# The experts' first product by seven block products, in three passes of 768 tokens

## The chip, the cores and the metric

The kernel runs on one core of one Trainium2 chip. The metric is the device time of one execution in microseconds (us). TensorE (PE in the profile) multiplies, with its weight loads listed as PEld; VectorE (DVE), ScalarE (ACT) and GpSimd (POOL) do the elementwise work; SyncE (SP) issues most of the DMAs.

## What is computed

Three layers run one after another on 2304 tokens (4 sequences of 576) of width 512. The reference, cut to what matters:

```python
# retention, 8 heads of 64
scores = q @ k.T / 8
x = (scores * where(rel >= 0, gamma[h] ** rel, 0)) @ v          # [2304, 512]
# first feed-forward (its weights come as float64)
h = x @ w_in                                                    # [2304, 1024]
e = exp(h - max(h)); sm = e / (sum(e) + 1e-9)
solu = h * sm
ln = (solu - mean) / sqrt(var + 1e-6) * g_ln
x = ln @ w_out                                                  # [2304, 512]
# second feed-forward, 4 experts, each w1 [512, 1024] and w2 [1024, 512]
for e in range(4):
    out += p[:, e] * (relu(x @ w1[e]) @ w2[e])
```

## The kernel before

Every large product keeps float32 accuracy with three matmuls in the float32r format: each operand is split into a high part (a copy rounded by ScalarE) and a low part (operand minus high part, on VectorE or GpSimd), and `mm3` (lines 99 to 103) issues high x high, high x low and low x high. TensorE loads a 128x128 stationary tile for each of them and streams 384 or 512 columns.

The tokens go in two halves of 1152 (9 groups of 128, 3 blocks of 384). For each half the stages are:

- Retention of a group (`att_*`): scores `att_qk` (line 262), decay mask `att_ret` (VectorE, line 269), keys x values `att_st` (279), running state `att_state` (VectorE, 296 and 298), outputs `att_pv` (314 to 325), split of the outputs `att_x`. Scaled values (line 231) and scaled queries (248, 249; for some groups of the opening on VectorE, 242) come before. The 1 MB of a group lies in one of two buffers (two more at the very start), and the load of group g+2 waits until the outputs of group g have read theirs.
- First projection of a group: `h_mm` (24 matmuls of 512 columns into `hps`), then `chain1` to `chain3` (maximum 356, exp 359, softmax and moments 368 and 372, norm 383), then eight transposes `t_mm` (403) with a split.
- `x2_mm`: for a block of 384 tokens and each of four 128-column pieces, 24 matmuls of 384 columns.
- The experts: in each of `nsteps` = 96 steps of a half, `l1` makes one 128-row piece of the hidden layer for one block (12 matmuls of 384 columns, relu and split on ScalarE 441 and VectorE 442), and `l2`, two steps behind, adds one piece to three output tiles (9 matmuls of 512 columns); after eight pieces `l2_out` scales by the expert's probability and adds to the sum (457, 459).

The float64 weights w_in and w_out are decoded in 16 chunks at the start (`dec_pre` on ScalarE 159 and 160, `dec_dve` on VectorE 164 to 172, `dec_pool` on GpSimd 176 and 177), split, and their float32 value is also stored to DRAM (`scr`, ScalarE's DMA queue), from where the second half loads and splits them again. The experts' weights are loaded and split in each half (`w_split`).

The order of the first part is written out by hand in `ORDER`: it covers the retention and the first projection of the first half and the decoding of all 16 chunks. The first `x2_mm` follows it. The second half's retention is spread between its first projections (`step`), with the first two groups inside the first half's last expert steps. Engines run their instructions in the order of the program. PSUM has two buffers of 1024 columns (`psA`: `hps`, the output tiles) and four of one bank (`psB`: everything else).

Of the kernel before, what the change touches and what calls it, by code (L numbers as in the profile page):

```python
# [10 lines left out]
F32R = mybir.dt.float32r  # L11
AF = mybir.ActivationFunctionType
# [11 lines left out]
HALF = NT // 2  # L24
GH = HALF // P
BLK = 384
NB = HALF // BLK
TB = BLK // P
KD = DM // P
KF = FF // P  # L30
NJ = 9
TABW = 1024 + 512 + NJ * H + NJ * NP + 128
U32 = mybir.dt.uint32
# [13 lines left out]
R0 R1 A0 P0 P1 C1 D0 A1 D1 G0 C0 K0 R2 G1 B0 A2 E0 E1 P2 V2 J0 v1 Q2 q1 K1 v0 R3 J1 R4 P3 S1 D2 S0 U0 G2 R5 O0  # L47
U1 K2 O1 D3 A3 X0 G3 J2 P4 e2 X1 S2 D4 E3 A4 G4 O2 Q3 U2 H0 K3 R6 X2 P5 V3 D5 P6 K4 R7 q4 J3 D6 G5 A5 R8 J4 V4
G6 H2 P7 S3 e4 S4 D7 V5 E5 U3 O3 E6 U4 O4 S5 X3 G7 P8 D8 Q5 X4 R9 E7 K5 H1 A6 R10 V6 P9 J5 O5 Q6 P10 U5 K6 N0
G8 H3 D9 S6 J6 X5 M0 G9 A7 O6 H4 C2 R11 K7 H5 N1 q7 M1 F0 U6 v7 S7 Z0 X6 E8 F1 E9 A8 I0 R12 J7 D10 O7 G10 Q8  # L50
P11 N2 U7 D11 v8 X7 T0 H6 K8 E10 S8 R13 G11 P12 H7 U8 P13 R14 M2 J8 I1 N3 O8 F2 D12 T1 X8 H8 H9 I2 M3 E11 F3
N4 D13 T2 H10 H11 P14 I3 M4 G12 N5 F4 M5 R15 D14 T3 G13 E12 H12 F5 I4 H13 N6 H14 P15 I5 M6 H15 D15 G14 G15 T4
F6 E13 E14 N7 E15 H16 M7 I6 F7 T5 I7 H17 N8 M8
# [4 lines left out]
def retention_solu_moe(  # L58
# [15 lines left out]
    wp = ctx.enter_context(tc.tile_pool(name="wp", bufs=8))  # L74
    stp = ctx.enter_context(tc.tile_pool(name="stp", bufs=2))
    drp = ctx.enter_context(tc.tile_pool(name="drp", bufs=1, space=bass.MemoryType.DRAM))
    bdp = ctx.enter_context(tc.tile_pool(name="bdp", bufs=2))
    ap2 = ctx.enter_context(tc.tile_pool(name="ap2", bufs=2))
    xp = ctx.enter_context(tc.tile_pool(name="xp", bufs=4))
    ep = ctx.enter_context(tc.tile_pool(name="ep", bufs=3))  # L80
    lp = ctx.enter_context(tc.tile_pool(name="lp", bufs=1))
    x2p = ctx.enter_context(tc.tile_pool(name="x2p", bufs=3))
    accp = ctx.enter_context(tc.tile_pool(name="accp", bufs=1))
# [13 lines left out]
    mhalf = const.tile([P, 1], F32, name="mhalf")  # L97

    def mm3(ps, lhs, rhs, first, last):
        (lh, ll), (rh, rl) = lhs, rhs  # L100
        nc.tensor.matmul(ps, lh, rh, start=first, stop=False)  # L101
        nc.tensor.matmul(ps, lh, rl, start=False, stop=False)  # L102
        nc.tensor.matmul(ps, ll, rh, start=False, stop=last)  # L103

    def split(dst_hi, dst_lo, src, scale=None):
        if scale is None:
            nc.scalar.activation(out=dst_hi, in_=src, func=AF.Copy)  # L107
            nc.vector.tensor_tensor(out=dst_lo, in0=src, in1=dst_hi.bitcast(F32), op=ALU.subtract)  # L108
        else:
            nc.scalar.activation(out=dst_hi, in_=src, func=AF.Copy, scale=scale)  # L110
            nc.vector.scalar_tensor_tensor(
                out=dst_lo, in0=src, scalar=scale, in1=dst_hi.bitcast(F32), op0=ALU.mult, op1=ALU.subtract
            )

# [1 line left out]
    scr = [drp.tile([P, 512], F32, name=f"scr{i}") for i in range(16)]  # L116
    mixed = [("A", 0), ("A", 1)] + [x for i in range(6) for x in (("A", i + 2), ("B", i))] + [("B", 6), ("B", 7)]
    worder = []
    for half in range(2):
        first = [("A", i) for i in range(8)] + [("B", i) for i in range(8)]  # L120
        for kind, i in first if half == 0 else mixed:
            worder.append((kind, scr[i] if kind == "A" else scr[8 + i]))
        for e in range(E):
            for kind, i in first if e == 0 else mixed:
                worder.append((kind, w1[e, i] if kind == "A" else w2[e, i]))
    wstate = {"dma": 0, "cut": 16}
    wstage = {}
    wtiles = {"A": {}, "B": {}}
    wcount = {"A": 0, "B": 0}
    dec = []  # L130

    def w_load():
        i = wstate["dma"]
        if i >= len(worder):
            return
        wstate["dma"] = i + 1
        if i < 16:
            if i == 0:
                dec.append(x2p.tile([P, 3072], F32, tag="x2", name="dec_raw"))
                dec.append(x2p.tile([P, 3072], F32, tag="x2", name="dec_w0"))  # L140
                dec.append(x2p.tile([P, 3072], F32, tag="x2", name="dec_w1"))
# [579 lines left out]
```

## Time and profile before

| | us |
|---|---|
| median of 3 runs (1137.45 to 1139.17) | 1137.88 |
| span of the profiled execution | 1137.7 |
| PE busy | 1102.1 (97%) |
| PEld busy | 990.7 (87%) |
| DVE busy | 452.4 (40%) |
| ACT busy | 327.2 (29%) |
| POOL busy | 98.9 (9%) |

Busy time is the time in which an engine has an instruction in execution. Matmuls overlap one another, so what one costs is read from the distance between starts, not from its duration. The timeline lists starts and durations, the chain of waits lists the pieces that set the end, the view by line groups instructions and gives the mean of one, and the view by stretches gives busy times, granted TensorE clock, DMA share and rate in a stretch.

### The profile page before, as it was taken

The page shows a single profiled execution, that of the slowest core. Times are in us where ns is not written, and L with a number is a line of the kernel's source. Part 1 is how long each engine was busy: PE and PEld are TensorE (multiplying, and loading weights), DVE is VectorE, ACT ScalarE, POOL GpSimd, SP SyncE. Part 2 cuts the span into 40 slices and gives each one's busy share as a digit, 9 for nine tenths or more (in the row PEclk, how much of TensorE's full clock was granted, in tenths as well). Part 3 has the DMA queues.
Part 4 walks back from the last instruction along what each step waited for, and adds up shares of the span by engine and source line. Part 5 has one row for each costly group of instructions (what it writes and reads, how often), then busy time and mean ns, then how long its engine had stood idle before and what let it go on. Part 6 is the DMA issues. An engine that isn't in the chain of part 4 may idle for free.

```text
span 1137.7 us, 14749 instructions
## 1 busy us (share of the span) xinstructions
PE 1102.1 (97%) x6176; PEld 990.7 (87%) x6176; DVE 452.4 (40%) x788; ACT 327.2 (29%) x613; POOL 98.9 (9%) x93
## 2 busy tenths in 40 slices
PE   4798999999999999999999999999999999999998
PEld 4676899999999999999877899999999999999997
DVE  6998743214223411432346635422431241233221
ACT  3456842113112311311134626311321131122110
POOL 4744500000000000000002200000000000000000
PEclk9899999999999999999999999999999999999999
DMA  8452012103101300211244300210220030021000
GB/s 327 178 211 76 38 48 68 35 1 111 37 1 38 111 1 1 94 55 65 84 149 158 112 1 11 84 56 1 74 74 1 19 112 19 1 74 57 28 29 28
DMA packets 31314, 75.82 MB, mean 67 GB/s; under 512 B 3728, under 2 KB 3728, under 8 KB 29072
## 3 DMA queue, kind: packets, MB, share of 16 engines
q1 hardware_dynamic: 28944, 70.69, 18.7%
q10 hardware_dynamic: 2304, 4.20, 1.0%
q8 instruction: 48, 0.79, 0.3%
q14 instruction: 18, 0.15, 0.0%
HBM read 65.96 MB, written 8.91 MB: 66 GB/s over the span
## 4 chain that ended last, share of the span: by engine, by line
PE 91%; DVE 7%; ACT 1%; POOL 0%; issue 0%; DMA 0%; POOLq 0%; DVEq 0%; ACTq 0%
PE l1ps L101 12%; PE l1ps L103 12%; PE o L102 12%; PE l1ps L102 12%; PE o L103 12%; PE o L101 12%; PE x2ps L101 3%; PE x2ps L102 3%; PE x2ps L103 3%; PE hps L101 2%; PE hps L102 2%; PE hps L103 2%; PE qk L262 1%; PE tps L403 1%; PE o L325 1%; PE o L314 1%
## 5 line engine op out<-in xcount | busy, mean ns | idle before, releaser
L442 DVE SCALAR_TENSOR_TENSOR hts<-l1ps,hts 128x384 fp32r<-128x384 f32 x192 | 107.0, 557 | 530.4 <-ACT hts L441 530.4
L441 ACT ACTIVATE hts<-l1ps 128x384 fp32r<-128x384 f32 x192 | 94.4, 492 | 608.8 <-PE l1ps L103 608.8
L103 PE MATMUL l1ps<-x,wA 128*128 128x384 f32 x768 | 258.9, 337 | 0.0
L101 PE MATMUL l1ps<-x,wA 128*128 128x384 f32 x768 | 258.7, 337 | 0.0
L102 PE MATMUL l1ps<-x,wA 128*128 128x384 f32 x768 | 257.9, 336 | 0.0
L103 PE MATMUL o<-wB,hts 128*128 128x512 f32 x576 | 227.8, 396 | 0.0
L102 PE MATMUL o<-wB,hts 128*128 128x512 f32 x576 | 227.4, 395 | 0.0
L101 PE MATMUL o<-wB,hts 128*128 128x512 f32 x576 | 224.0, 389 | 0.0
L101 PEld LDWEIGHTS l1ps<-x,wA 128*128 128x128 f32 x768 | 144.3, 188 | 8.3 <-issue 0.2
L102 PEld LDWEIGHTS l1ps<-x,wA 128*128 128x128 f32 x768 | 144.1, 188 | 7.8
L103 PEld LDWEIGHTS l1ps<-x,wA 128*128 128x128 f32 x768 | 144.0, 188 | 0.0
L103 PEld LDWEIGHTS o<-wB,hts 128*128 128x128 f32 x576 | 108.0, 188 | 23.0
L102 PEld LDWEIGHTS o<-wB,hts 128*128 128x128 f32 x576 | 108.0, 188 | 18.4
L101 PEld LDWEIGHTS o<-wB,hts 128*128 128x128 f32 x576 | 108.2, 188 | 17.5
L101 PE MATMUL hps<-wA,xt 128*128 128x512 f32 x144 | 60.1, 417 | 1.5 <-ACT hps L372 1.1
L102 PE MATMUL hps<-wA,xt 128*128 128x512 f32 x144 | 57.3, 398 | 0.0
L103 PE MATMUL hps<-wA,xt 128*128 128x512 f32 x144 | 57.2, 397 | 0.0
L108 DVE TENSOR_TENSOR wA<-wst,wA 128x512 fp32r<-128x512 f32 x72 | 49.6, 691 | 14.7 <-ACT wA L107 14.5
L108 DVE TENSOR_TENSOR wB<-wst,wB 128x512 fp32r<-128x512 f32 x72 | 51.1, 709 | 8.8 <-ACT wB L107 8.2
L231 POOL TENSOR_TENSOR grp<-grp,tabs 128x512 f32<-128x512 f32 x11 | 12.1, 1103 | 428.6 <-DMA grp<-in_qkv 428.6
L107 ACT ACTIVATE wA<-wst 128x512 fp32r<-128x512 f32 x72 | 44.8, 626 | 13.2 <-DMA wst<-in_w 6.6
L107 ACT ACTIVATE wB<-wst 128x512 fp32r<-128x512 f32 x72 | 45.1, 627 | 10.8 <-DMA wst<-in_w 7.3
(100 smaller groups left out, 1086.4 us busy)
## 6 DMA issues: line engine op xcount, KB each, us to landing
wst<-in_w SPq DMA_DIRECT2D x128, 256.0 KB, 2.6
grp<-in_qkv SPq DMA_DIRECT2D x15, 1024.0 KB, 5.0
dec_raw<-in_w_in SPq DMA_DIRECT2D x8, 512.0 KB, 6.0
scr<-dec_w ACTq DMA_DIRECT2D x16, 256.0 KB, 2.5
dec_raw<-in_w_out SPq DMA_DIRECT2D x8, 512.0 KB, 4.3
wst<-scr SPq DMA_DIRECT2D x16, 256.0 KB, 2.6
out<-accA SPq DMA_DIRECT2D x12, 256.0 KB, 2.0
lend<-in_qkv SPq DMA_DIRECT2D x2, 1024.0 KB, 8.1
```

The lines of the kernel that those rows point to most:

```text
L101: nc.tensor.matmul(ps, lh, rh, start=first, stop=False)
L102: nc.tensor.matmul(ps, lh, rl, start=False, stop=False)
L103: nc.tensor.matmul(ps, ll, rh, start=False, stop=last)
L107: nc.scalar.activation(out=dst_hi, in_=src, func=AF.Copy)
L108: nc.vector.tensor_tensor(out=dst_lo, in0=src, in1=dst_hi.bitcast(F32), op=ALU.subtract)
L231: eng.tensor_tensor(out=vd, in0=v, in1=vtab[:, j].unsqueeze(2).to_broadcast([P, H, 64]), op=ALU.mult)
L262: nc.tensor.matmul(qk[a][:, n], kt[r, n], qt[r, n], start=True, stop=True)
L314: nc.tensor.matmul(o[r, n, 0:cross], v[:, 2 * n + a], ret[:, a, n, 0:cross], start=n == 0, stop=j == 0 and n == NP - 1)
L325: nc.tensor.matmul(o[:, n, 0:cross], st[:, n], qd[:, n, 0:cross], start=False, stop=n == NP - 1)
L403: nc.tensor.transpose(ps[:, f], y[:, (4 * u + f) * P : (4 * u + f + 1) * P], ident)
L441: nc.scalar.activation(out=ht[:, 0], in_=ps, func=AF.Relu)
L442: nc.vector.scalar_tensor_tensor(out=ht[:, 1], in0=ps, scalar=0.0, in1=ht[:, 0].bitcast(F32), op0=ALU.max, op1=ALU.subtract)
```

## The change

The tokens go in three passes of 768 (6 groups, two blocks of 384 tokens, b = 0 and 1).

- Experts' first product: the product x @ w1 of a pass is cut into 2x2 blocks (512 hidden inputs in two halves, tokens in two blocks, hidden units m and m+4) and made by seven block products instead of eight, with sums and differences of blocks. The blocks of w1 are laid out in advance (a21, a11, a12, a22); GpSimd makes four combined blocks s1 to s4 of each step (`w1_ops`), ScalarE and VectorE or GpSimd split everything. The four combined blocks of x (T1 to T4) are made behind `x2_mm`. The seven products of a step share three PSUM tiles x, y and z; partial sums are copied out by ScalarE (t1r, t2r, t5r) and added by VectorE.
- A step has 7 products of 6 matmuls (384 columns); an expert has 4 steps, then all of `l2` for six output tiles (24 matmuls of 512 columns each).
- `ORDER` now holds the retention of all 18 groups, the decoding of all 16 chunks and the first projection of 6 groups. The outputs of groups 6 to 17 are split and stored to DRAM (`att_store`, SP queue, 512 KB each) and loaded in their pass.
- The decoded weights are stored as two parts (512 KB a chunk instead of 256 KB) after the low part is made, and loaded again as parts in passes 1 and 2 (`next_loads`, and eight loads of wB). All low parts of decoded weights, all scaled values and the second factor of all scaled queries are on GpSimd; none of them is on VectorE.
- w2 is split by ScalarE and GpSimd inside the steps, w1 mostly behind `l2`.

```diff
+NPASS = 3
+GP = NG // NPASS
+TB = GP // 2
...
+    def low(dst, src, hi, eng=None):
+        (eng or nc.vector).tensor_tensor(out=dst, in0=src, in1=hi.bitcast(F32), op=ALU.subtract)
...
+    def dec_lo(i):
+        t = dec_out(i)
+        low(t[:, 1], dec_views(i)[4], t[:, 0], nc.gpsimd)
+
+    def dec_store(i):
+        nc.scalar.dma_start(out=(s_in if i < 8 else s_out)[i % 8], in_=dec_out(i).bitcast(F32))
...
+    def grp(g):
+        return grps[:, 3072 * (g % 2) : 3072 * (g % 2) + 3072]
...
+    def att_store(g):
+        if g >= GP:
+            nc.sync.dma_start(out=s_x[g], in_=att_to(g).bitcast(F32))
...
+    PRODUCTS = {1: (A11, B11), 2: (A12, B21), 3: (S4, B22), 4: (A22, T4), 5: (S1, T1), 6: (S2, T2), 7: (S3, T3)}
...
+    def prod(s, i, bank, more=False):
+        a, b = PRODUCTS[i]
+        for kk in range(2):
+            mm3(
+                bank, (wpart(s, a, kk, 0), wpart(s, a, kk, 1)), (xpart(b, kk, 0), xpart(b, kk, 1)),
+                not more and kk == 0, kk == 1, more,
+            )
...
+        if i == 1:
+            prod(s, 1, x)
+            copy(t1r, x)
+            if m > 0:
+                relu_hi(1, m + 3, c22)
+                relu_lo(1, m + 3, c22)
+        elif i == 5:
+            prod(s, 5, y)
+            copy(t5r, y)
+        elif i == 2:
+            prod(s, 2, z)
+            add(z, z, t1r)
+        elif i == 6:
+            prod(s, 6, x, True)
+            copy(t2r, x)
+            relu_hi(0, m, z)
+            relu_lo(0, m, z)
+        elif i == 3:
+            prod(s, 3, y, True)
+            add(y, y, t2r)
+        elif i == 7:
+            prod(s, 7, x, True)
+            add(c22, x, t5r)
+            relu_hi(1, m, y)
+            relu_lo(1, m, y)
...
+        elif i == 4:
+            prod(s, 4, x, True)
+            relu_hi(0, m + 4, x)
+            relu_lo(0, m + 4, x)
...
+            for m in range(NM):
+                s = s0 + m
+                for i in (1, 5, 2, 6, 4, 3, 7):
+                    if i != 4:
+                        l1(s, i)
+                    elif m > 0:
+                        l1(s - 1, 4)
...
+            for b in (1, 0):
+                for t in range(TB):
...
+                    l2_out(p, e, b * TB + t, ps)
+                    run(bg, 6)
```

In the new `ORDER` the letters are: R, A, C loads; P, D, G, E, e decoding and split of a weight chunk, W its store; V, Q, q, K, J, S, U, O, X, x the retention of a group and y its store; H, N, n, M, m, F, f, I, T, t, u first projection, norm and transposes. Its last part is the retention of groups 14 to 17 and the transposes of groups 3 and 4.

## Rows read from the trace of the kernel before

**Rows 1.** The page: span, and busy time of each engine.

```profile
span 1137.7 us, 14749 instructions
PE 1102.1 (97%) x6176; PEld 990.7 (87%) x6176; DVE 452.4 (40%) x788; ACT 327.2 (29%) x613; POOL 98.9 (9%) x93
```

**Rows 2.** Timeline of PE in an expert step: start us, duration us, instruction.

```profile
300.43 0.39 PE L101 MATMUL o<-wB,hts 128*128 128x512 f32 x1
...
302.51 0.33 PE L101 MATMUL l1ps<-x,wA 128*128 128x384 f32 x1
...
304.62 0.39 PE L101 MATMUL o<-wB,hts 128*128 128x512 f32 x1
```

**Rows 3.** Stretches: from:to length, busy us (instructions) per engine, clock, DMA.

```profile
0.00:133.40 133.40, 103.80 (x764) 85.65 (x765) 115.16 (x202) 75.65 (x132) 72.26 (x65) 0.94 0.48 175
30.00:60.00 30.00, 22.31 (x199) 18.66 (x197) 29.46 (x41) 12.86 (x26) 20.52 (x16) 0.79 0.51 178
180.00:570.00 390.00, 390.00 (x1998) 353.74 (x1997) 116.84 (x191) 79.49 (x155) 2.25 (x2) 1.00 0.16 50
```

**Rows 4.** Chain of waits: start us, us, what; opening, then a group of the second half.

```profile
59.46 0.43 PE hps L102
...
98.99 0.87 PE tps L403 x8
...
100.10 0.23 PE hps L102
...
600.17 1.09 PE qk L262 x16
601.26 0.62 PE st L279 x16
...
604.86 1.02 PE o L314 x16
605.89 1.09 PE o L325 x8
...
609.73 1.09 PE qk L262 x16
```

**Rows 5.** By line, opening to 133.4 us, DVE: instruction xcount | busy us, mean ns.

```profile
L269 DVE TENSOR_TENSOR ret<-qk,tabs 128x512 f32<-128x512 f32 x18 | 11.5, 680 | 0.0
L368 DVE SCALAR_TENSOR_TENSOR ex<-hps,rs,ex 128x1024 f32<-128x1024 f32 x8 | 10.3, 1284 | 0.3
L356 DVE TENSOR_REDUCE nm<-hps 128x1 f32<-128x1024 f32 x8 | 9.7, 1218 | 2.3 <-PE hps L103 2.2
L242 DVE SCALAR_TENSOR_TENSOR grp<-grp,tabs 128x128 f32<-128x128 f32 x12 | 6.3, 583 | 0.0
L298 DVE TENSOR_TENSOR st<-st,st 64x256 f32<-64x256 f32 x12 | 5.0, 418 | 0.1
```

**Rows 6.** Stretches, DVE's instructions on the decoding's tile alone: busy us (instructions).

```profile
5.00:7.05 2.05, 1.92 (x5) 1.00 0.89 278
0.00:133.40 133.40, 52.74 (x70) 0.94 0.48 175
```

**Rows 7.** Timeline of all engines, 7 to 9 us.

```profile
7.16 1.31 POOL L176 TENSOR_TENSOR dec_w<-dec_w 128x512 f32<-128x512 f32 x1 [5.41 <-DVE dec_w L172]
7.26 1.49 DVE L166 TENSOR_SCALAR dec_w<-dec_raw 128x512 uint32<-128x512 uint32 x1
```

**Rows 8.** By line, opening to 133.4 us, POOL.

```profile
L195 POOL TENSOR_TENSOR wB<-dec_w,wB 128x512 fp32r<-128x512 f32 x7 | 9.0, 1291 | 14.2 <-ACT wB L194 14.2
L249 POOL TENSOR_TENSOR grp<-grp,tabs 128x512 f32<-128x512 f32 x3 | 4.0, 1340 | 0.2 <-ACT grp L248 0.2
```

**Rows 9.** DMA issues of the opening: KB each, us from issue to landing.

```profile
grp<-in_qkv SPq DMA_DIRECT2D x6, 1024.0 KB, 6.1
```

**Rows 10.** Timelines of DVE and ACT, one group's norm in the second half.

```profile
690.27 1.23 DVE L356 TENSOR_REDUCE nm<-hps 128x1 f32<-128x1024 f32 x1 [1.75 <-PE hps L103]
697.48 0.19 ACT L372 ACTIVATION_READ_ACCUMULATOR hps<-ex,mu 128x1 f32 x1
```

**Rows 11.** The page: the costliest group of DVE, the hidden layer's low part.

```profile
L442 DVE SCALAR_TENSOR_TENSOR hts<-l1ps,hts 128x384 fp32r<-128x384 f32 x192 | 107.0, 557 | 530.4 <-ACT hts L441 530.4
```

More of the change, by code (lines that the diff above doesn't have):

```diff
@@ L116, in retention_solu_moe @@
[L116 to L141, printed above, removed]
[L142 to L147 removed]
+    states = [const.tile([P, NP, P], F32, name=f"st{i}") for i in range(2)]
@@ new lines, in retention_solu_moe, with mm3 @@
+    s_in = [drp.tile([P, 1024], F32, name=f"sin{i}") for i in range(8)]
+    s_out = [drp.tile([P, 1024], F32, name=f"sout{i}") for i in range(8)]
+    s_x = [drp.tile([P, 1024], F32, name=f"sx{i}") for i in range(NG)]
+    def mm3(ps, lhs, rhs, first, last, more=False):
+        (lh, ll), (rh, rl) = lhs, rhs
+        nc.tensor.matmul(ps, lh, rh, start=first, stop=False, skip_group_check=more)
+        nc.tensor.matmul(ps, lh, rl, start=False, stop=False, skip_group_check=more)
+        nc.tensor.matmul(ps, ll, rh, start=False, stop=last, skip_group_check=more)
@@ new lines, in t_to, with t_hi, t_lo, tr @@
+    def t_to(g, part, u):
+        b, j = divmod(g % GP, TB)
+        return hT[b][:, part, 4 * u : 4 * u + 4, j * P : (j + 1) * P]
+    def t_hi(g):
+        for u in range(2):
+            copy(t_to(g, 0, u), tps[g][u])
+    def t_lo(g):
+        for u in range(2):
+            low(t_to(g, 1, u), tps[g][u], t_to(g, 0, u))
+    def tr(g):
+        t_mm(g)
+        t_hi(g)
+        t_lo(g)
+    B11, B21, B22, T1, T2, T3, T4 = range(7)
+    def xpart(b, kk, part):
+        return xv[0][:, b, kk, part] if b < 4 else xv[1][:, b - 4, kk, part]
@@ L487, in weights, with l2_mm @@
-    def weights(kind, at):
-        return {i: wtiles[kind].get(at + i) for i in range(8)}
+            nc.vector.scalar_tensor_tensor(out=a, in0=ps, scalar=sc, in1=a, op0=ALU.mult, op1=ALU.add)
+        if e == E - 1:
+            nc.sync.dma_start(out=out[tok * P : (tok + 1) * P, :], in_=a)
+    FORDER = [0, 4, 1, 5, 2, 6, 3, 7]
+    def l2_mm(ps, b, t, fs, first, last):
+        sl = slice(t * P, t * P + P)
+        for f in fs:
+            h, w = hT[b], wB[:, f]
+            mm3(
+                ps, (h[:, 0, f, sl], h[:, 1, f, sl]), (w[:, 0], w[:, 1]),
+                first and f == fs[0], last and f == fs[-1],
+            )
@@ new lines, in retention_solu_moe @@
+        for atom in ORDER.split():
+            atoms[atom[0]](int(atom[1:]))
+        second(0, None)
+        experts(0)
+        for p in range(1, NPASS):
+            g0 = p * GP
+            for i in range(8):
+                nc.sync.dma_start(out=wB[:, i].bitcast(F32), in_=s_out[i])
+            for i in range(GP):
+                g = g0 + i
+                h_mm(g, 0)
+                h_mm(g, 1)
+                chain1(g)
+                chain1e(g)
+                if i > 0:
+                    chain3a(g - 1)
+                if i > 1:
+                    tr(g - 2)
+                if i > 0:
+                    chain3m(g - 1)
+                    chain3b(g - 1)
+                chain2(g)
+                chain2s(g)
+            second(p, g0)
+            experts(p)
```

664 lines of the change are left out of this document (302 added, 362 removed).

## The prediction, made before the change was built

> **What bounds the kernel now.** I read the page first: TensorE is busy for 1102.1 of 1137.7 us, every other engine for under half of it apart from its own weight loads [rows 1]. Busy time does not say what a matmul costs, so the next view is the timeline of an expert step: the nine 512-column matmuls from 300.43 to 302.51 take 2.08 us, 0.231 each, the twelve 384-column ones from 302.51 to 304.62 take 2.11, 0.176 each, with no gap [rows 2]. The stretches come third: from 180 to 570 us TensorE is busy in all of 390 us at full clock while VectorE has 116.8 and GpSimd 2.3 [rows 3]. So after the opening the time is the sum of the matmul distances, and a matmul left out is 0.176 us won. The opening, up to the first `x2_mm` at about 133.4 us, is another stage: TensorE is busy for 103.8 us (overlaps counted once) and VectorE for 115.2 of 133.4 [rows 3]; from 30 to 60 us VectorE has 29.5 of 30 while TensorE has 22.3 at a granted clock of 0.79. There VectorE sets the pace.
>
> **The change, part by part.** The sum is made against the span of 1137.7 us, which stands 0.2 us below the median of the runs.
>
> *Matmuls left out.* Before, a hidden piece of a block takes 12 matmuls, 192 pieces, 2304 in all. After, 3 passes x 4 experts x 4 steps x 7 products x 6 = 2016 of the same shape, with a new stationary tile for each as before. 288 x 0.176 = -50.6 us. The second products, `x2_mm`, first projections and transposes keep their number and shape.
>
> *Work that changes sides of the opening's end.* Retention costs TensorE 1.09 + 0.61 + 1.02 + 1.09 = 3.81 us a group at full clock [rows 4]. The last nine groups leave the PE-bound second half for the opening: -34.3 after it. Three first projections of 24 matmuls at 0.23 and one set of transposes of 0.87 [rows 4] go the other way: +16.6 + 0.9. With the matmuls left out, what comes after the opening shrinks by 50.6 + 34.3 - 17.5 = 67.4 us. All else hangs on how long the opening gets.
>
> *The opening's length.* VectorE's 115.2 us change as follows [rows 5]: 18 more masks at 0.68 (+12.2), 9 more low parts of outputs, also 128x512 from PSUM, at the same 0.68 (+6.1), 16 more state updates at 0.42 (+6.7); gone are twelve scaled-query instructions (-6.3), three scaled values and six low parts of weights, 128x512 again (-6.1), and two groups' maximum and softmax at 1.22 and 1.28 (-5.0). Net +7.6, 122.8 us. GpSimd gets what VectorE lost and more: 11 scaled values and 11 query products at 1.34, 7 low parts at 1.29 [rows 8], 72.3 + 38 = 110 us.
> That matters because VectorE's decoding instructions get longer beside GpSimd: an L166 that starts during a GpSimd instruction takes 1.49 us [rows 7], while the first chunk's four, with nothing beside them, take 1.92 together. All DVE work on the decoding's tile is 52.7 us [rows 6]; less the six low parts, 48.6, against 16 x 1.92 = 30.7 alone: 17.9 us of waiting at a GpSimd share of 72.3/133.4 = 0.54. With 110 us in about 150 the share is 0.73 and the waiting 24.2: +6.3, so VectorE has 129.1. Bounds: no added waiting, or every one of the 64 instructions 1.01 longer than alone (1.49 against a quarter of 1.92), 65 of waiting, +47; I take the scaled value, since the share is the only thing that changes.
> Before, the opening lasted 133.4/115.2 = 1.158 times VectorE's work (it starts late and ends with a chain). Kept, this gives 149.5 us. `ORDER` now ends with the last groups' chain with little beside it, scores, mask and outputs of some 4 us of which part is extra: I add 3. Opening: 153 us, against 133.4: +19.6.
> (The Trainium skill, page "SBUF — State Buffer", section "Who interferes with whom", says that the engine that comes second is blocked for the whole of the other's instruction. Rows 7 agree. By it alone, an estimate: 64 instructions x 0.73 x half of a 1.3 us instruction = 30 us of waiting instead of 24, and the sum would be 7 us higher, 1104.)
>
> *What else could set the opening.* ScalarE has 75.7 us before; 44 more short query copies and 9 output copies, all taken at 0.68 or less, make at most 112. Each W on its queue now waits for GpSimd's low part (1.29) with the Q and X copies queued behind it: 16 x 1.29 = 21 at most, 133, still under 153; I take none of it on the path, and all of it in the range. DMA: 0.48 of the engines carried 175 GB/s, 23 MB [rows 3]; 9 more groups (9.4 MB), larger weight stores (4.2) and 12 output stores (6.3) make some 43 MB, at 175/0.48 = 365 GB/s 118 us: covered, but no longer idle. TensorE has 106 us of work at full clock (18 x 3.81, 6 x 24 x 0.23, 5 x 0.87). On SP's queue each load of group g+2 waits for the outputs of g, and R loads and y stores stand behind it; who waits for them is the decoding and the reuse of the two output buffers (a rival below).
>
> *The expert steps.* Each step of 7.39 us holds 7 ScalarE passes and 7 VectorE passes over 384 columns, at 0.56 [rows 11] 3.9 us each, and per expert splits and adds of w1 and w2: about three quarters of either engine at most, with GpSimd under half. The tightest wait is x: two PSUM buffers, so the first product of step s+1 needs the low part of x of step s-1, which follows product 4 by one ScalarE and one VectorE pass, 1.12 us, while products 3 and 7 take 2.11. The other tiles have two products or more of room. No row shows such a chain: between 0 and a 0.6 us stall in each of 48 steps (29 us); I take 2, because before the same eviction pair never held TensorE up [rows 3] and the room is twice the pass.
>
> *Pass starts.* The norm of a group holds its `hps` for 7.4 us (690.27 to 697.67 [rows 10]) plus some tenths to the maximum's start, and with two buffers TensorE wants it back after one projection and two transposes, 5.53 + 2 x 0.87 = 7.27: 0.4 us in each of 8 groups without retention between them, +3. Before, retention filled that. The reloads (7.3 MB at 365 GB/s, 20 us) lie under the last expert's second products (6 x 24 x 0.231 = 33 us); bare they would cost up to 20 a pass. The chain behind the last `x2_mm` to product 6 (some five VectorE passes at 0.56 against three products of 1.06) is covered within a microsecond: +2 for three passes. The second split of w_in and w_out goes away, hidden before, worth nothing.
>
> Sum: 1137.7 - 67.4 + 19.6 + 2 + 3 + 2 = 1096.9, so **1097 us**.
>
> **The rivals.**
> *B, the groups set the opening.* Retention runs through two buffers. In the second half a group took 609.73 - 600.17 = 9.56 us [rows 4], there with TensorE full; a load takes 6.1 us to land [rows 9], and load, scores, mask and outputs with two or three waits in order of some 3 us make 17 to 19 for a pair of buffers, 8.5 to 9.5 a group. At 9.5: 8 + 18 x 9.5 = 179, +26: 1123. For it: the last part of `ORDER` is nothing but groups. Against: 153 us needs 8.1 a group, not far.
> *C, the products wait.* If GpSimd's 1.3 us instructions get in the way of the x chain, some 0.5 us in each of 48 steps: +24, 1121. For it: GpSimd had 2.3 us in 390 of expert time and now has some 13 in the 30 of an expert's steps (eight low parts at 1.3, four half-size sums). Against: the instructions on that chain read PSUM, and the masks, which do so too, average 0.68 beside a busy GpSimd [rows 5].
> *D, slower: the loads stand in SP's queue.* Each group load sits behind R loads and y stores that wait for VectorE. If that adds 4 us to each load's way, a pair takes 23 us, a group 11.5, the opening 8 + 207 = 215: +62, 1159. It decides from 10.3 us a group on (opening 194): then all is eaten. Against: rows 3 show DMA at 0.48 and the other engines with room.
> *E, TensorE at the lower clock.* At a granted clock of 0.79 a projection matmul took 0.43 instead of 0.23 [rows 4], the 1.2 GHz level. With 106 us of work in 153, TensorE has gaps. Were it low throughout, 106 would become about 190, and TensorE would set the opening: 1137. Against: the mean was 0.94 in the opening before, and a TensorE that falls behind has no gaps. (The Trainium skill, page "TensorE: Matmul & The Clock Gate", section "What's actually happening", has the low level as the default that activity lifts, which speaks against packing an opening with small pieces; rows 3 show both levels.)
> That the change leaves out less than it says is no case: the products are counted from the code.
>
> **How the numbers follow.** My forecast 0.62, B 0.18, C 0.09, D 0.07, E 0.04. The forecast's own range is 1077 (opening 122.8 + the 18.2 us that VectorE was idle = 141, no stalls) to 1112 (opening 165, stalls of 10). Leaving D and E out (0.11), the range takes in B and C: 1077 to 1127. A difference of 0.2% is about what a measurement can tell. Forecast, B and C are faster: 0.89; E is split, half faster or slower and half the same: same 0.02, slower 0.08, faster 0.90.
>
> **What would show it.** Right: the first `x2_mm` near 153 us, VectorE over 80% busy until then, L164 to L172 longer than before; seven products in 7.4 us and no idle time ahead of l1x, l1y, l1z; about 323 us from one pass's first projection to the next (144 x 0.23 + 6 x 0.87 + 864 x 0.176 + 576 x 0.231). Wrong: the first `x2_mm` past 165 with VectorE waiting for loads (B, D), idle time of PE ahead of product 1 or 7 released by VectorE (C), a granted clock under 0.8 up to there (E). My number falls with the opening's length above all: each microsecond there is one in the total.

## The result and the profile after

The changed kernel takes **1091.34 us** (median of five runs, 1089.67 to 1095.52) beside 1137.88 for the kernel before: a ratio of 0.9591, 95% interval 0.9572 to 0.961. The forecast was 1097 in a range of 1077 to 1127. The profiled execution of after is the slowest of its five: 1095.52 us, with a span of 1093.3. The spans of the other four are 1087.5 to 1089.5, so what is read from this one trace may be some 4 us longer than usual.

The page of after, span and busy time, against [rows 1]. TensorE has 288 instructions fewer and is busy for 55 us less; GpSimd's work has grown fourfold.

```profile
span 1093.3 us, 15079 instructions
PE 1047.1 (96%) x5888; PEld 941.3 (86%) x5888; DVE 565.1 (52%) x947; ACT 471.1 (43%) x901; POOL 393.5 (36%) x399
```

Timeline of TensorE in after, against [rows 2]: one expert step, from its first product to the next step's, and then one whole tile of second products (start us, duration us, instruction).

```profile
270.07 0.33 PE L129 MATMUL l1x<-xb,wA 128*128 128x384 f32 x1
...
277.35 0.33 PE L129 MATMUL l1x<-xb,wA 128*128 128x384 f32 x1
```

```profile
236.21 0.39 PE L129 MATMUL o<-wB,h 128*128 128x512 f32 x1
...
241.65 0.39 PE L129 MATMUL o<-wB,h 128*128 128x512 f32 x1
```

The step's 42 matmuls take 7.28 us, 0.173 each, with no gap. The tile's 24 take 5.44 us, 0.227 each, where [rows 2] had 0.231.

Stretches of after, against [rows 3]: from:to length, busy us (instructions) of PE, PEld, DVE, ACT and POOL, granted clock, DMA share, GB/s. The first `x2_mm` starts at 163.6 us, so the first row is the whole opening.

```profile
0.00:163.60 163.60, 124.35 (x1177) 102.97 (x1177) 131.19 (x211) 89.74 (x178) 105.87 (x93) 0.89 0.72 257
30.00:60.00 30.00, 24.93 (x280) 20.38 (x278) 28.42 (x36) 15.23 (x35) 26.62 (x21) 0.94 0.82 291
180.00:440.00 260.00, 259.58 (x1325) 237.16 (x1324) 120.64 (x196) 103.64 (x203) 89.96 (x93) 1.00 0.28 94
```

In the first expert stage (third row) TensorE is busy for 259.6 of 260 us at full clock. The time in which it stood idle from the first `x2_mm` to the end, by what ended it (us in total, times, longest), is 3.2 us in all:

```profile
PE tps L389 <- ACT acc L380: 1.4, 2, 0.7
PE hps L129 <- ACT hps L363: 1.1, 4, 0.3
PE l1y L129 <- ACT tmp L137: 0.7, 2, 0.4
```

To see where the 44.4 us between the two spans went, I added up the distances from each matmul's start to the next one's over both traces, from the first `x2_mm` to the end of the last matmul, 3.7 us before the end of either span. A stall counts with the matmul ahead of it.

| part, us | before | after | difference | predicted |
|---|---|---|---|---|
| opening, to the first `x2_mm` | 132.8 | 163.6 | +30.8 | +19.6 |
| first products | 404.2 | 352.2 | -52.0 | -50.6, +2 (steps) and +2 (behind the last `x2_mm`) |
| retention | 32.7 | 0 | -32.7 | -34.3 |
| first projections | 52.3 | 67.2 | +14.9 | +16.6 |
| transposes | 9.5 | 11.4 | +1.9 | +0.9 and +3 for pass starts |
| `x2_mm` | 100.6 | 102.4 | +1.9 | 0 |
| second products | 401.9 | 392.7 | -9.2 | 0 |
| after the opening, in all | 1001.2 | 926.0 | -75.2 | -60.4 |

The +1.9 of `x2_mm` is two waits of the transposes for a norm, which count with the `x2` matmul ahead of them (0.87 us each, at 487.8 and 809.2). The opening cost 11 us more than forecast and the rest gave 15 more; that the two nearly cancel in the total is luck.

Now the opening itself. First VectorE's instructions on the decoding's tile, against [rows 6], columns as in the stretches with only the engines that touch the tile (DVE, ACT, POOL); then groups of DVE and POOL by line (xcount | busy us, mean ns | idle before and what ended it), against [rows 5] and [rows 8]; then the group loads, against [rows 9].

```profile
0.00:163.60 163.60, 56.42 (x64) 34.62 (x56) 62.83 (x48) 0.89 0.72 257
```

```profile
L249 DVE TENSOR_TENSOR tmp<-qk,tabs 128x512 f32<-128x512 f32 x36 | 23.1, 681 | 4.7 <-DMA tabs<-in_tab 2.9 <-PE qk L241 1.8
...
L273 DVE TENSOR_TENSOR st<-st,st 64x256 f32<-64x256 f32 x24 | 10.0, 418 | 0.9 <-PE st L259 0.6
L314 DVE SCALAR_TENSOR_TENSOR wA<-o,wA 128x512 fp32r<-128x512 f32 x12 | 8.2, 685 | 6.5 <-ACT wA L307 6.4
```

```profile
L232 POOL TENSOR_TENSOR grps<-grps,tabs 128x512 f32<-128x512 f32 x16 | 22.0, 1374 | 9.0 <-ACT grps L227 9.0
...
L217 POOL TENSOR_TENSOR grps<-grps,tabs 128x512 f32<-128x512 f32 x16 | 18.2, 1137 | 17.5 <-DMA grps<-in_qkv 14.5 <-PE o L300 2.9
```

```profile
grps<-in_qkv SPq DMA_DIRECT2D x17, 1024.0 KB, 6.9
```

VectorE's work is 131.2 us, within 2% of the 129.1 forecast, and the masks, state updates and low parts cost per instruction what they did in [rows 5]. The decoding takes 56.4 us (forecast 54.9), GpSimd has 105.9 (110). So the amounts were right. What was not right is the opening that follows from them: 163.6/131.2 = 1.247, not 1.158. VectorE stood idle for 32.4 us instead of 18.2, and 13.4 of that lie behind 120 us.

The end of the opening, from the last group's scores on (timeline of all engines):

```profile
152.44 1.16 PE L241 MATMUL qk<-grps 64*128 64x128 f32 x16
...
153.13 2.37 ACT L380 ACTIVATE acc<-acc,mu,rstd 128x1024 f32<-128x1024 f32 x2 [1.46 <-DVE ve L369]
...
155.41 0.57 ACT L307 ACTIVATE wA<-o 128x512 fp32r<-128x512 f32 x1
155.89 1.26 ACT L227 ACTIVATE grps<-grps,tabs 128x128 f32<-128x128 f32 x4
156.02 0.69 DVE L314 SCALAR_TENSOR_TENSOR wA<-o,wA 128x512 fp32r<-128x512 f32 x1 [2.09 <-ACT wA L307]
156.62 1.28 DVE L249 TENSOR_TENSOR tmp<-qk,tabs 128x512 f32<-128x512 f32 x2
...
157.36 0.43 PE L289 MATMUL o<-tmp,grps 128*64 128x128 f32 x2 [3.76 <-DVE tmp L249]
...
159.19 2.08 PE L300 MATMUL o<-grps,st 128*128 128x128 f32 x8
...
163.59 0.45 PE L129 MATMUL x2ps<-h,wB 128*128 128x384 f32 x1
```

The scores of group 17 are done at 153.6, but ScalarE is in the norms of groups 4 and 5 (L380, 2.37 us). Behind these in the order of the program stands the high part of group 16's output (155.41); VectorE's low part of it (156.02) waits for that, and group 17's mask (156.62) stands behind the low part. TensorE waits 3.76 us for the mask, does the outputs, then two groups' transposes, and only then begins with x2: 11.2 us from the scores to the first `x2_mm`. After that pause the cross product `o` of eight matmuls (L300) takes 2.08 us; [rows 4] have 1.09 for eight matmuls of the same kind. The granted clock of that stretch (the first figure behind the busy times) is 0.50, the lower of the clock's two levels, 1.2 GHz:

```profile
159.10:161.30 2.20, 2.20 (x11) 2.11 (x11) 0.00 (x0) 0.00 (x0) 0.00 (x0) 0.50 0.00 0
```

(The Trainium skill, page "TensorE: Matmul & The Clock Gate", section "What's actually happening", calls the slow clock the default and says that activity releases it; the 2.08 behind a pause of 3.8 us agrees.)

### The profile page after: what moved, and what is told of

Read it like the earlier page. It is cut to its first block, busy times and chain, and to the rows that moved or that the text cites. A ratio compares the mean times of both kernels' runs of the same rounds, so it can differ in the third digit from the quotient of the medians.

```text
span 1093.3 us, 15079 instructions
## 1 busy us (share of the span) xinstructions
PE 1047.1 (96%) x5888; PEld 941.3 (86%) x5888; DVE 565.1 (52%) x947; ACT 471.1 (43%) x901; POOL 393.5 (36%) x399
## 4 chain that ended last, share of the span: by engine, by line
PE 84%; DVE 8%; DMA 3%; ACT 2%; issue 1%; POOL 1%; SPq 0%; ACTq 0%; DVEq 0%
PE o L131 12%; PE o L130 12%; PE o L129 12%; PE l1x L129 6%; PE l1x L130 6%; PE l1x L131 6%; PE l1y L129 3%; PE l1y L130 3%; PE l1y L131 3%; PE x2ps L129 2%; PE x2ps L130 2%; PE x2ps L131 2%; PE hps L129 2%; PE hps L131 2%; PE hps L130 2%; PE l1z L130 1%
## 5 line engine op out<-in xcount | busy, mean ns | idle before, releaser
L131 PE MATMUL o<-wB,h 128*128 128x512 f32 x576 | 224.5, 390 | 0.0
L130 PE MATMUL o<-wB,h 128*128 128x512 f32 x576 | 224.4, 390 | 0.0
L129 PE MATMUL o<-wB,h 128*128 128x512 f32 x576 | 224.0, 389 | 0.0
L469 POOL TENSOR_TENSOR tmp<-tmp 128x256 f32<-128x256 f32 x192 | 154.2, 818 | 187.5 <-DVE wA L134 164.1
L134 POOL TENSOR_TENSOR wB<-tmp,wB 128x512 fp32r<-128x512 f32 x96 | 123.8, 1295 | 239.9 <-ACT wB L137 237.1
L137 ACT ACTIVATE wA<-tmp 128x768 fp32r<-128x768 f32 x144 | 98.7, 701 | 173.2 <-DMA tmp<-in_w 108.3
L131 PEld LDWEIGHTS o<-wB,h 128*128 128x128 f32 x576 | 108.1, 188 | 22.4
L130 PEld LDWEIGHTS o<-wB,h 128*128 128x128 f32 x576 | 108.1, 188 | 22.0
L129 PEld LDWEIGHTS o<-wB,h 128*128 128x128 f32 x576 | 108.1, 188 | 21.7
L134 DVE TENSOR_TENSOR wA<-tmp,wA 128x768 fp32r<-128x768 f32 x144 | 108.1, 773 | 0.9 <-ACT wA L137 0.9
L129 PE MATMUL l1x<-xb,wA 128*128 128x384 f32 x288 | 96.6, 336 | 0.0
L130 PE MATMUL l1x<-xb,wA 128*128 128x384 f32 x288 | 96.3, 334 | 0.0
L131 PE MATMUL l1x<-xb,wA 128*128 128x384 f32 x288 | 96.2, 334 | 0.0
L137 ACT ACTIVATE wB<-tmp 128x512 fp32r<-128x512 f32 x96 | 60.6, 632 | 12.0 <-DMA tmp<-in_w 11.8
L129 PE MATMUL l1y<-xa,wA 128*128 128x384 f32 x192 | 64.5, 336 | 0.7 <-ACT tmp L137 0.7
L129 PE MATMUL x2ps<-h,wB 128*128 128x384 f32 x192 | 64.9, 338 | 0.1
L131 PE MATMUL x2ps<-h,wB 128*128 128x384 f32 x192 | 64.2, 334 | 0.0
L130 PE MATMUL x2ps<-h,wB 128*128 128x384 f32 x192 | 64.2, 334 | 0.0
L131 PE MATMUL l1y<-xa,wA 128*128 128x384 f32 x192 | 64.1, 334 | 0.0
```

What stands on the lines that cost most here:

```text
L129: nc.tensor.matmul(ps, lh, rh, start=first, stop=False, skip_group_check=more)
L130: nc.tensor.matmul(ps, lh, rl, start=False, stop=False, skip_group_check=more)
L131: nc.tensor.matmul(ps, ll, rh, start=False, stop=last, skip_group_check=more)
L134: (eng or nc.vector).tensor_tensor(out=dst, in0=src, in1=hi.bitcast(F32), op=ALU.subtract)
L137: nc.scalar.activation(out=dst, in_=src, func=AF.Copy)
L469: return lambda: nc.gpsimd.tensor_tensor(out=dst, in0=a, in1=b, op=op)
```

## The experiments

All start from the changed kernel. The table has the first `x2_mm` and what comes after it from each profiled execution, and the device times; those with an interval are medians of four or five runs.

| kernel | first `x2_mm`, us | after it, us | time, us | ratio to before |
|---|---|---|---|---|
| after | 163.6 | 926.0 | 1091.34 | 0.9591 (0.9572 to 0.961) |
| e1, product 2 twice | 164.1 | 973.6 | 1143.64, one run | |
| e2, no group loads | 158.0 | 925.9 | 1089.78, one run | |
| e11, e2 timed | 161.3 | 927.6 | 1093.64 | 0.9604 (0.959 to 0.9617) |
| e3, no GpSimd decoding | 152.0 | 926.3 | 1083.78, one run | |
| e6, less VectorE decoding | 153.6 | 926.1 | 1085.33, one run | |
| e12, e6 timed | 154.1 | 925.5 | 1085.31 | 0.9534 (0.9521 to 0.9547) |
| e7, e2 and e6 | 143.9 | 926.4 | 1075.82, one run | |
| e10, four group buffers and e4 | 157.3 | 927.2 | 1087.68 | 0.9555 (0.9539 to 0.9572) |
| e4, the end put in another order | 153.7 | 927.0 | 1087.81 | 0.9563 (0.9538 to 0.9588) |
| e5, tiles in pairs | 159.7 | 955.8 | 1121.43, one run | |
| e8, tiles in threes | 165.2 | 995.9 | 1167.02, one run | |
| e9, threes, wide buffer | 157.3 | 999.8 | 1163.41, one run | |

What comes after the opening is 925.5 to 927.6 us wherever it isn't edited (e4 and e10 move two transposes there). So of the 6 us by which executions of one kernel differ some 2 at most lie behind the opening. At the median after's opening would be about 163.6 - 4.2 = 159.4 us (an estimate: profiled time less median time).

### What a product is worth: e1

```diff
             prod(s, 2, z)
+            prod(s, 2, z, True)
```

> The changed kernel with an eighth product of 6 matmuls in each of the 48 steps: product 2 is issued twice, the second time added to the same tile, so the hidden layer is not the reference's. Theory: a product costs its matmul distances and nothing else, 288 x 0.174 = +50.1 us on the span of 1093.3, to 1143 us. Rival: the steps are held by the copies, relus and adds between the products, and an added product fills waits: under +40 us, below 1133.

Measured: what follows the opening grew by 47.6 us, 0.165 for each of the 288 matmuls. At the same time 2.2 us of stalls at the start of the three passes' experts went away (1.5 of them at `l1x`); with these an added matmul costs 0.173, its distance. The saving of seven products for eight is thus TensorE's time, matmul by matmul, and no other engine's limit stood behind it.

### What sets the opening: e2, e3, e6 and e7

Two theories for the 11 us that were missing: V, that VectorE alone paces the opening and lost more to its neighbours; L, that the groups' loads do.

```diff
 # e2 and e11
     def att_load(g):
+        if g >= 2:
+            return
 # e3
-        nc.gpsimd.tensor_tensor(out=x, in0=x, in1=mag, op=ALU.mult)
-        nc.gpsimd.tensor_tensor(out=x, in0=x, in1=bits, op=ALU.add)
+        return
 # e6 and e12
-        nc.vector.tensor_scalar_min(out=mag, in0=mag, scalar1=F64_MAX)
...
-        nc.vector.scalar_tensor_tensor(
-            out=bits, in0=mag, scalar=3, in1=bits, op0=ALU.logical_shift_left, op1=ALU.bitwise_or
-        )
 # e7: e2 and e6 together
```

> The changed kernel without the loads of groups 2 to 17: they work on the data of groups 0 and 1 again. What set the opening of 163.6 us (from the start to the first x2 matmul)? Theory V (VectorE's work, in the order of the program): the opening stays within 3 us of 163.6. Theory L (loads through two buffers): it falls by 10 us or more, to 153 or below, and PE and VectorE wait less for scores.

> The changed kernel without GpSimd's two decoding instructions of each of the 16 chunks (42 us of GpSimd), so the decoded weights are wrong. Theory V: VectorE's decoding falls from 56.4 us towards 16 x 1.92 = 31, to about 42, and the opening by about as much, to near 150 us. Theory L: VectorE's decoding falls too, but the opening stays within 4 us of 163.6.

> The changed kernel without two of VectorE's four decoding instructions of each chunk (the clamp and the shift, 29.8 us by their means), so the decoded weights are wrong. Theory V: the opening falls by 25 us or more, to 139 or below. Theory L: by under 8 us, to 156 or above, and VectorE just waits longer.

> Loads of groups 2 to 17 left out and two of VectorE's four decoding instructions left out, as in the two runs that did one of these (opening 158.0 and 153.6 us instead of 163.6); decoded weights and outputs are not the reference's. Theory of two limits (whichever of loads and VectorE is relieved, the other holds the opening at nearly the same length): the opening falls by more than the 5.6 + 10.0 of the two runs together, to 145 or below. Rival (a third thing, the program's order on PE and the four PSUM buffers, holds it): by less than their sum, to 149 or above.

e3's decoding on VectorE, in the view of the stretches for the decoding's tile (DVE, ACT, POOL):

```profile
0.00:152.00 152.00, 38.24 (x64) 34.38 (x56) 20.70 (x16) 0.93 0.78 277
```

Leaving out 42 us of GpSimd's instructions takes 18.2 us from VectorE's same 64 (56.42 to 38.24). That is the waiting which the prediction had worked out from [rows 6, 7]: it put 24.2 us on the opening, and 56.4 less the 30.7 of the instructions alone gives 25.7. (The Trainium skill, page "SBUF — State Buffer", section "Who interferes with whom", has the second engine blocked for the whole of the other's instruction where a VectorE instruction uses the port pair shared with GpSimd; the estimate by it was 30 us, so the measurement lies between, nearer to the scaled row.)

But neither e3 nor e6 turns what it takes from VectorE into time. The opening of e2 (158.0) and of e6 (153.6) lies between what the two theories had said. In e3 and e6 it fell by 11.6 and 10.0 us on the traces, which is 6 to 7.6 in time against after's median. Since one run can't tell 3 us here, e2 and e6 were timed again; e12's trace then says where the rest went.

### The same, timed: e11 and e12

> e2 again, timed in five rounds (the loads of groups 2 to 17 left out, so what the retention computes is not the reference's). The changed kernel's own five runs spread from 1089.7 to 1095.5 us, and its profiled execution is the slowest of them, so that one look at e2 (1089.8) can't tell a gain. Theory of two limits: median 1085 to 1089, a ratio to the kernel before of 0.953 to 0.957 against 0.9591. Rival, that no group's load is on the path and all of e2's gain was one execution's luck: median 1089.5 to 1092, a ratio of 0.957 or more.

> e6 again, timed in five rounds (VectorE's clamp and shift of the decoding left out, some 27 us of its work in the opening, so the projections' weights are wrong). Theory of two limits: median 1082 to 1087, ratio 0.950 to 0.955, a third of the work taken away at most. Rival, that VectorE alone sets the opening: median under 1075, ratio under 0.945.

e11 is not faster than after: 0.9604 against 0.9591. That is what the rival in its expectation had said: the single run of e2 had shown a gain that isn't there, and theory L falls as a limit by itself. e12 gains 6 us (1091.34 to 1085.31) for 26.4 us of VectorE's work taken away (131.19 to 104.77 in the opening), so theory V falls too. The chain of waits from 20 to 140 us, shares by line, of after, of e11 and of e12:

```profile
by line: PE o L289 8.7%; DMA grps<-in_qkv 7.9%; DVE dec L165 7.0%; DMA tmp<-in_w_in 7.0%; DVE dec L168 6.5%; PE qk L241 6.1%; DVE tmp L249 6.1%; PE o L300 5.5%; DVE dec L163 4.4%; PE hps L129 4.3%; PE hps L131 3.8%; PE hps L130 3.8%; DVE de
```

```profile
by line: DVE tmp L251 9.2%; DVE dec L168 9.1%; PE o L291 8.1%; DVE dec L165 8.0%; PE o L302 7.3%; DVE dec L163 6.5%; issue 6.5%; DVE st L275 4.2%; DVE dec L171 3.7%; DVE acc L356 3.3%; PE hps L129 3.2%; PE qk L243 2.7%; PE st L261 2.7%; PE 
```

```profile
by line: DMA grps<-in_qkv 35.0%; PE o L285 6.2%; PE qk L237 4.9%; PE hps L129 4.5%; PE o L296 4.3%; PE hps L131 3.8%; PE hps L130 3.8%; POOL dec L171 3.4%; POOL grps L213 3.2%; POOL dec L172 3.2%; DVE tmp L245 3.2%; ACT grps L223 3.0%; issu
```

Without loads the chain goes through VectorE's decoding and the time is the same. With VectorE's work lightened the loads fill 35% of it, where they had 7.9. The loads stand just behind VectorE's work. Only with both gone, in e7, does the opening fall to 143.9 us, 19.7 less than in after's trace; e7's time is 15.5 us under after's median, in one run. What is left then in the middle of the opening is TensorE. The stretch from 80 to 120 us in e12 and in e7, columns as above:

```profile
80.00:120.00 40.00, 35.52 (x366) 29.09 (x366) 31.66 (x60) 28.83 (x55) 27.18 (x24) 1.00 0.79 283
```

```profile
80.00:120.00 40.00, 39.11 (x359) 31.94 (x357) 34.27 (x62) 31.68 (x62) 29.28 (x26) 1.00 0.41 146
```

TensorE has 39.1 of 40 us there in e7. So three limits follow each other within some 20 us of the opening: VectorE's work, the loads, TensorE.

### Two more buffers for the groups: e10

```diff
     def grp(g):
+        if g < 8 and g % 4 > 1:
+            return spare[:, 3072 * (g % 2) : 3072 * (g % 2) + 3072]
...
-    h1 = big.tile([P, 2, KF, BLK], F32R, name="h1")
+    spare = big.tile([P, 6144], F32, tag="h1", name="spare")
```

`A2` to `A9` stand up to two groups earlier in `ORDER`, `h1` is taken from the same place ahead of `T0`, and e4's edits (below) are in it.

> e4 with two more buffers for the retention groups 2 to 7: until the first transposes the place of the first hidden half is empty, so groups 2, 3, 6 and 7 lie there, and the loads of groups 2 to 9 are issued two groups sooner; every other load and all the work stay. Theory of two limits (loads of groups and VectorE's work, each hiding the other): the waits for groups shrink from some 56 us (23.9, 16.8 and 15.8 in e4) by a third or more, the opening falls from e4's 153.7 us by 2 to 5, no more than the 5.6 that leaving the loads out gave, total 1083 to 1086. Rival, that the transfers stand against the engines' capacity (42 MB in 154 us) and not for want of a free buffer: opening within 1 us of e4's, total 1087 to 1089; and if the sooner loads push the weights' loads back in SP's queue, 2 to 4 us later than e4.

The waits did shrink. The largest one from 40 to 80 us in after, and VectorE beside it, then the same stretch of e10 (its largest wait is no longer one for a load; the stretch's columns as above):

```profile
ACT grps L227 <- DMA grps<-in_qkv: 17.1, 5, 4.8
```

```profile
40.00:80.00 40.00, 34.41 (x343) 28.45 (x343) 36.54 (x48) 19.79 (x44) 33.80 (x26) 0.92 0.80 296
```

```profile
ACT wA L309 <- PE o L302: 7.0, 2, 5.4
```

```profile
40.00:80.00 40.00, 34.76 (x341) 28.65 (x342) 37.85 (x49) 19.61 (x43) 33.48 (x27) 0.87 0.69 245
```

The 17 us of waiting for loads (15.5 in e4, on which e10 is built) are gone and nothing is won: 1087.68 us beside e4's 1087.81. Over the whole opening ScalarE's waits for groups fell from 23.9 us in e4 to 1.3. (The first `x2_mm` of e10's trace is 3.6 us later than e4's, but that run was 3.4 us above its median, so the traces can't tell the two apart.) ScalarE had waited beside a VectorE that was busy for 36.5 of 40 us. The expectation's total of 1083 to 1086 was missed, and the rival's reason was not the right one either: the loads came sooner, so the transfers were not at their limit; they were not on the path. This agrees with e11.

### The end of the opening: e4

```diff
-F5
-f5 O16 F4 I5 f4 I4 K17 X16 Q17 x16 J17 q17 O17 Y0 X17 x17 y17 y16 T3 T4 t3 t4 u3 u4
+O16
+K17 X16 Q17 x16 J17 q17 F4 F5 f4 I4 f5 I5 O17 Y0 X17 x17 y17 y16
...
+            if p == 0 and m < 2:
+                tr(GP - 3 + m)
             if m == 2:
```

The norms of groups 4 and 5 go behind the last group's mask, and the transposes of groups 3 and 4 behind the first two `x2_mm`.

> The changed kernel with a new end of the opening: the norms of groups 4 and 5 go behind the mask of the last group, and the transposes of groups 3 and 4 behind the first two x2 products, which need groups 0 to 2 alone. Theory O (the end of the opening is a chain set by this order: the last group's output split, queries and mask stand behind two norms of 1.24 us on ScalarE and their waits on VectorE): the first x2 matmul comes 5 to 7 us earlier, the total falls by 4 to 5 us (the transposes' 1.7 us come later), ratio to the kernel before 0.955. Rival (the last group's load sets the end): under 1.5 us.

The same end in e4, to be laid beside that of after:

```profile
149.24 1.16 PE L241 MATMUL qk<-grps 64*128 64x128 f32 x16 [0.54 <-DMA grps<-in_qkv]
...
150.40 1.29 DVE L249 TENSOR_TENSOR tmp<-qk,tabs 128x512 f32<-128x512 f32 x2 [0.35 <-PE qk L241]
...
152.76 1.16 PE L300 MATMUL o<-grps,st 128*128 128x128 f32 x8
...
153.68 0.42 PE L129 MATMUL x2ps<-h,wB 128*128 128x384 f32 x1
```

From the scores to the first `x2_mm` it takes 4.4 us instead of 11.2. The mask follows the scores by 1.16 us instead of 4.18, and TensorE, with a pause of 0.75 instead of 3.76, is at full clock: the L300 row has 1.16, not 2.08. Of these 6.8 us the medians show 3.5 (1091.34 to 1087.81), a little under the 4 to 5 expected. The two intervals overlap, so the times alone do not show a gain over after; that e10, which has the same end, gives 1087.68 speaks for it. The kernel is faster than before, and likely the better of the two by about 3.5 us.

### Why a second product became shorter: e5, e8 and e9

A second product took 0.231 us on average before and 0.227 after, 6.9 of the 9.2 us (the rest was a stall of 2.4 before). Before, three token tiles take turns with three matmuls each; after, each tile is finished in one go. Does taking turns cost?

```diff
 # e5 (e8: three tiles of a half in turn; e9: two of the three in one wide buffer)
-            for b in (1, 0):
-                for t in range(TB):
...
+            for pair in (((1, 0), (1, 1)), ((1, 2), (0, 0)), ((0, 1), (0, 2))):
...
+                for k, f in enumerate(FORDER):
+                    for i, (b, t) in enumerate(pair):
...
+                        l2_mm(two[i], b, t, [f], k == 0, k == KF - 1)
```

> The changed kernel with the second products of two output tiles interleaved: after every three matmuls the next three go to the other tile's PSUM bank, as before the change, where nine matmuls went to three banks in turn. Why did the 512-column matmuls go from 0.2326 us to 0.2272? Theory P (changing the bank costs some 0.01 us): the mean distance returns to about 0.231, +6 to +7 us in all. Rival (it comes from the l1 matmuls in between or from other engines' work): the distance stays at 0.227 and the time within 2 us.

> Read for the distance between starts of the second products' matmuls, which is 231 ns in the kernel before (229, 233, 236 inside each three, and 227 flat only where a tile is finished in one go) and 227 in the changed kernel. Here the three token tiles of a half take turns, three matmuls each, as before the change, each in a PSUM buffer of its own (e5 did that with two tiles). Theory P1, that taking turns among three accumulators costs: 231 to 233 ns on the mean of 1728, 392.7 becomes 399 to 402 us. Theory P2, that it needs the two halves of one wide PSUM buffer: 227 here. Theory P3, that the cost lies in the first products between: 227 here too. The time itself is to be longer in any case, by 20 to 60 us, since three tiles are evicted at once and the next half and the next first products wait for their buffers, as in e5.

> The same three tiles taking turns, but two of them in the two halves of one wide PSUM buffer, as the kernel before has them. P1: 231 to 233 ns, as e8. P2: 231 to 233 ns, where e8 has 227. P3: 227 in both. The time is longer, 20 to 60 us, for the same waits as in e8.

The 1728 matmuls take 392.7 us in e5, 392.9 in e8 and 392.7 in e9: 0.227 in all three. Taking turns costs nothing. The trace of before has both distances within its last tiles (timeline of PE):

```profile
1117.41 0.39 PE L101 MATMUL o<-wB,hts 128*128 128x512 f32 x1
...
1119.49 0.39 PE L101 MATMUL o<-wB,hts 128*128 128x512 f32 x1
...
1124.93 0.39 PE L101 MATMUL o<-wB,hts 128*128 128x512 f32 x1
```

Nine matmuls in turns, straight behind first products, take 2.08 us, 0.231 each; the 24 of the next tile 5.44, 0.227. The trace of after has both within one tile that is finished in one go (timeline of PE, from the first second product behind first products on):

```profile
229.37 0.39 PE L129 MATMUL o<-wB,h 128*128 128x512 f32 x1
...
231.45 0.39 PE L129 MATMUL o<-wB,h 128*128 128x512 f32 x1
...
233.49 0.39 PE L129 MATMUL o<-wB,h 128*128 128x512 f32 x1
```

The first nine take 2.08 us here too, without any turns, and the next nine 2.04. The distances are the same at each of the 12 such places of after, of e5, of e8 and of e9: 0.231 on average over the first nine matmuls behind first products, 0.227 from the tenth on. So what costs is the change from first products to second ones, 0.04 us each time. Before, there were 184 such changes, after there are 24 (two at each of the 12 places), which makes some 6.4 us of the 6.9. The way back costs too: twelve first products straight behind second ones take 2.105 us (2.11 in [rows 2]) and twelve within a long row 2.08. Why a change costs this is open.

What follows the opening is longer by 30 us in e5, 70 in e8 and 74 in e9. For e5 at most 7 us had been expected, for e8 and e9 20 to 60, for evictions that come together. In e5 TensorE stood idle for 20.2 us at `l1y` for ScalarE (11 times) over the whole run, and behind some of these pauses the first products stand 0.320 us apart instead of 0.173, at the lower level (granted clock 0.66 from 263 to 268 us), which is the rest of the loss. One such place, first in e5 (timelines of SP, DVE, ACT and PE), then the same load and split in after:

```profile
258.25 0.90 SPq L487 DMA_DIRECT2D tmp<-in_w  x2
258.33 0.75 DVE L568 TENSOR_SCALAR acc<-o,pr 128x512 f32<-128x512 f32 x1
...
262.02 0.63 ACT L137 ACTIVATE wB<-tmp 128x512 fp32r<-128x512 f32 x1 [3.53 <-DMA tmp<-in_w]
262.56 0.47 ACT L137 ACTIVATE tmp<-l1y 128x384 f32<-128x384 f32 x1
...
263.08 0.44 PE L129 MATMUL l1y<-xa,wA 128*128 128x384 f32 x1 [2.06 <-ACT tmp L137]
```

```profile
257.51 0.91 SPq L487 DMA_DIRECT2D tmp<-in_w  x2
260.89 0.75 DVE L568 TENSOR_SCALAR acc<-o,pr 128x512 f32<-128x512 f32 x1 [3.22 <-PE o L131]
...
262.40 0.62 ACT L137 ACTIVATE wB<-tmp 128x512 fp32r<-128x512 f32 x1
```

It was not the eviction. In after the load of the next expert's second weights is issued 3.4 us before the last tile is evicted (257.51, 260.89); in e5 it goes out with it (258.25, 258.33). By the program this is because a batch of background work is issued behind each finished tile, and the pairs finish late. The load lands at 262.0, the split at the head of ScalarE's queue waits 3.53 us for it, and the copies of `l1y` and `l1x` stand behind the split. The traces of e5 have this at all nine places where TensorE waits for over 2 us. e8 and e9 wait for ScalarE's copies at `l1y` and `l1x`, 42 and 46 us in all: at `l1y` behind the same split, which waits 3.0 to 3.3 us for its load, and at `l1x` behind splits of w1 that wait 7.6 to 8.7 us for GpSimd's combined blocks. Rival C had products wait too, though for another reason. In after the split at the place shown has no wait.

## Why the prediction came out right

**The matmuls left out** were right: -50.6 forecast, and e1 prices them back at 47.6 and the 2.2 of stalls that it covers. The reading of [rows 2] (no gap, so the time is the sum of distances) is what carried the forecast. The -52.0 measured has three parts: 288 x 0.173 is 49.9, fewer changes between kinds of products gave 4.3 more, and 2.2 us of stalls came on top, nearly all where the first steps of a pass begin.

**Work that changes sides** was right within 2 us a term: retention -32.7 for -34.3, projections +14.9 for +16.6, transposes +1.9 for +0.9.

**Stalls** were put at 7 us: 2 in the steps, 3 at the pass starts, 2 behind the last `x2_mm`. TensorE idles for 3.2 us in after, but a start that comes late while the matmul ahead is still listed as running does not show as idle time. By the distances between starts 7.6 us are lost against the same matmuls in a long row: 0.2 in the steps, 5.1 in projections, transposes and `x2_mm`, nearly all at the two later pass starts, 2.3 behind the last `x2_mm` of the passes. So the sum was right and the parts were not quite. From one pass's first projection to the next it took 321.4 us (446.4 to 767.8) for the 323 forecast. Rival C did not come about in the changed kernel.

**Second products** were the first step that failed. The prediction said that they "keep their number and shape" and costed the change at nothing. The change also puts their order from nine in a step to 24 in a tile, with 24 changes from first products in place of 184, and -9.2 us followed (2.4 of it a stall of before that is gone). The rows that would have told it stood in the trace of before, from 1117.41 to 1124.93 us.

**The opening's length** was the second, and it is a mis-sized term, not a wrong mechanism: 153 us forecast, 163.6 in the trace, about 159.4 at the median. VectorE's work (129.1 forecast, 131.2), its waiting beside GpSimd (24.2, 25.7) and GpSimd's work (110, 105.9) were right. The ratio of 1.158, "it starts late and ends with a chain", was carried over, and three microseconds were added for the end. Measured, VectorE idled 14.2 us more than in the opening before. e4 shows where 6.8 of them in the trace (3.5 in the median) went: into the end, where the last mask stood behind two norms on ScalarE, and the first `x2_mm` behind two sets of transposes on TensorE. The rest of the 14.2 no run places on one cause. And a ratio to VectorE's work can't be the law: it was 1.247 in after, 1.47 in e12 (154.1/104.77), since other limits stand close behind.

**Rival B**, that the groups set the opening, was the nearest: a group took (152.4 - 8.4)/17 = 8.5 us in after from scores to scores, the lower end of its 8.5 to 9.5, against the 8.1 of the forecast. Yet its reason was not the one: without loads (e11) and with four buffers (e10) the time stayed. **Rival D** needed 11.5 us a group and fell with it. **Rival E** was seen in part: the granted clock was 0.89 in the opening instead of 0.94, and the end's pause put TensorE on the lower level; TensorE did not set the pace of after's opening, where it was busy for 124.4 of 163.6 us.

So the span came out 3.6 us under the sum (1093.3 for 1096.9) because two errors, +11 in the opening and -15 behind it, went against each other, and the median lies 2 us under the span. That closeness is luck; the range held both errors.

Some small slips of the prediction change nothing in this: the first `x2_mm` of before starts at 132.8 us, not 133.4; the 1.92 of [rows 6] has 0.04 us of a fifth instruction in it; the lower end of the range comes to 1078 by its own terms, not 1077; and 106 us at 0.43 for 0.23 would be 198, not 190, which puts rival E at 1142.

## What to carry to other kernels

Where the trace shows one engine's instructions without a gap, cost a change there by the distance of the very order that it will have, and look for that order elsewhere in the same trace: how often one kind of matmul follows another can cost something too. For a stage in which several engines are near full, a ratio to the busiest one's work says little about what taking work away brings: take two suspected limits away together before a limit is named. Work that is issued behind finished tiles carries the next stage's loads, so a new order of tiles moves these loads too.

## What the runs showed that was not expected

A 128x512 matmul with a new stationary tile each time costs 0.227 us in a long row and 0.231 over the first nine behind matmuls of 384 columns (2.08 us against 2.04 for nine), whether one tile is finished in one go or tiles take turns, and taking turns among two or three accumulators is free (392.7, 392.9 and 392.7 us for 1728). Executions of one kernel differ by 6 us (1089.67 to 1095.52), and what follows the opening by only 2 (925.5 to 927.6 over the kernels in which it is the same). And 17 us of waits for loads on ScalarE (e10) or all loads (e11) could go without a change in time, while the same loads were 35% of the chain as soon as VectorE had 26 us less to do (e12).
